# Expert weights loaded by halves over more rounds, and expert rows gathered three ahead, in a sparse-attention and MoE kernel

## The chip, the core and the metric

The kernel runs on one core of one Trainium2 chip. The metric is the device time of one execution in microseconds (us). A profile is one execution; its span begins with the first instruction, and all moments below are us from there. The engines are TensorE (PE, with its weight loads as PEld), VectorE (DVE), ScalarE (ACT), GpSimd (POOL) and SyncE (SP). SP, ACT and POOL issue DMAs, each on queues of its own.

## The reference

Attention over 4 batches of 8 heads, 768 positions of 64. Keys are cut into 24 chunks of 32; each query keeps the 6 chunks with the highest bound, and the result feeds a layer of 8 experts of which each token takes one, at most 80 tokens per expert.

```python
ub = np.sum(np.maximum(q[:, :, :, None, :] * k_min[:, :, None, :, :],
                       q[:, :, :, None, :] * k_max[:, :, None, :, :]), axis=-1)
ub = np.where(causal, ub, -1e9)                       # whole chunks ahead of the query
top_chunks = np.argsort(ub, axis=-1)[..., -6:]
scores = np.where(sel & (pos[:, None] >= pos[None, :]), scale * q @ k.T, -1e9)
x = (softmax(scores) @ v), heads side by side         # 3072 tokens x 512
expert_idx = np.argmax(x @ w_gate, axis=1); gate_w = probs[expert_idx]
for e in range(8):                                    # the 80 tokens with the highest gate
    out[tok_idx] = gate_w[tok_idx, None] * (np.maximum(x[tok_idx] @ w1[e], 0) @ w2[e])
```

Tokens that are dropped have zero rows in `out`.

## The kernel before

**Rounds.** The 32 heads are 8 quads of 4. A quad has 6 rounds, one for each pair of 128-key blocks against a third (256) of the queries, so the attention is 48 rounds, `for rd in range(N + 1)` with `g, r = divmod(rd, 6)`. In a round `score` puts scores into PSUM on PE (L459, and L463 for the chunk penalty), `exps` takes the exponential on ACT (L474), and on diagonal blocks POOL applies the causal mask (L479). On the other rounds (`summed`) POOL adds the two key blocks' exponentials into `both` (`sum_pairs`, L503). `value` multiplies by v (L492), `denom` sums (L517). Both belong to the round before, so PE has the next scores to work on while ACT and POOL are at it. After the last round of a query third `evacuate`, `gate_rows`, `scales` and `rows` divide and compute the gate logits, and `store` writes rows of x to a buffer in DRAM (`x_dram`).

**Bounds.** Each quad prepares the next: keys and queries are transposed on DVE (L264), the chunk minima and maxima taken (L281), keys reordered by POOL (L289), and in round r = 3 (round 4 in the first quad) `bound_all` issues 128 small matmuls (L390) for the bounds, of which `rank_all` makes the penalty. Keys and values of a quad to come are loaded by SP, its queries by ACT.

**Order of work.** The whole loop is under `tc.manual_schedule` for all engines: each engine's instructions run in the order in which the program writes them. In a round POOL has the mask or the pair sum, then what `flush` brings, then the expert weights due in that round, then the preparation steps. ACT issues zero fills of `out` after its exponentials.

**Weights.** Each expert has w1 (512 x 1024) and w2 (1024 x 512) in float32; a POOL DMA casts each to bf16 on the way (1024 KB written to SBUF). Eleven matrices, experts 0 to 4 and w1 of expert 5, go to tiles of their own, in the rounds of `whole_at`, by `load_whole` through `load_parts` (L153). The other five are loaded in rounds 40 to 44 by `late_weights`, in pieces, into tiles that the attention needs no more: `kn`, `qn` (round 40), `kT`, `qT` (41), `qp` (42), `QB`, `KB` (43), `vn` (three pieces, 44). POOL's loads use eight completion counters in turn.

**Zero fills.** `out` is filled with zeros by 12 DMAs of 512 KB (L139) in the rounds of `fills`.

**Experts.** After the selection of each expert's 80 tokens (steps of `freeze` and `weigh`, from round 44 on; the last indices come at L1003 to L1017), the second part of the kernel runs with only PE's order by hand. The lists of POOL, DVE and ACT are left to the scheduler there. POOL gathers the 80 rows of each expert from `x_dram` (L1232, one indirect DMA per expert, all eight first); `turn_rows` transposes them on PE (L1241) and copies them to SBUF on ACT (`XT`, L1244); `hidden` is 32 matmuls (L1255), whose first half goes through the relu on DVE (L1258), the second on ACT (L1261), both into `HT`; `result` is 8 matmuls (L1269), scaled by the gate on DVE (L1272) and scattered to `out` by POOL (L1274). The loop has PE run hidden(e), turn_rows(e+1), result(e-1).

Of the kernel before, what the change touches and what calls it, by code (L numbers as in the profile page):

```python
# [9 lines left out]
BF16 = mybir.dt.bfloat16  # L10
# [3 lines left out]
P = 128  # L14
# [11 lines left out]
NEXP = 8  # L26
DFF = 1024
# [9 lines left out]
def kernel(  # L37
# [11 lines left out]
    nc = tc.nc  # L49
# [93 lines left out]
    weights = {}  # L143
# [9 lines left out]
            nc.gpsimd.dma_start(out=dst, in_=src[:, c0:c0 + n, :])  # L153
            parts += [dst[:, c, :] for c in range(n)]

    def load_whole(e, which):
        w = wpb[which].tile([P, 4 * DFF], BF16, name=("w1", "w2")[which])
        load_parts(e, which, [w[:]])

    NQUAD = NBH // 4  # L160
    THIRD = 2 * P
# [43 lines left out]
    with tc.tile_pool(name="small", bufs=2) as small, \  # L205
# [853 lines left out]
        steps_of = {2: ["K0"], 3: ["K1", "Q0", "Q1"], 6: ["K0", "K1"], 7: ["Q0"], 8: ["Q1"]}  # L1059
        for g in range(2, NQUAD - 1):  # L1060
            steps_of.update({6 * g - 1: ["K0"], 6 * g: ["K1"], 6 * g + 1: ["Q0"], 6 * g + 2: ["Q1"]})
        fills = {11: 1, 17: 1, 23: 1, 29: 1, 45: 2, 46: 3, 47: 3}
        filled = list(range(sum(fills.values())))
        assert len(filled) == NTOK // (2 * P)
        whole_at = (2, 5, 10, 16, 22, 28, 34, 35, 36, 37, 40)
        ends = {}
        fz = freeze()
        frozen = {(N - 4, 2), (N - 4, 1), (N - 3, 1), (N - 2, 0), (N - 2, 1), (N - 1, 0)}
        with tc.manual_schedule(engines=set(mybir.EngineType) - {mybir.EngineType.Unassigned}):
            first, others = slice(0, 2), slice(2, QBLK)  # L1070
            load(0, k4, "kn", first)
            load(0, q4, "qn", first, nc.scalar)
            nc.scalar.activation(out=minus1[:], in_=crow[:], func=mybir.ActivationFunctionType.Exp,
                                 scale=1e-3)
            load(0, k4, "kn", others)
            load(0, q4, "qn", others)
            load_v(0, first)
            nc.sync.dma_start(out=wg_sb[:], in_=moe_w_gate.rearrange("(t r) e -> r t e", r=P))
            load_k(1)
            load_v(0, others)  # L1080
            load_q(1)
            load_v(1)
            idle(24)
            nc.gpsimd.memset(PEN[0][:], 0.0)
            build_indicator(cand[1][:, 0:SEQ])
            u = prep(0)
            units = [u]
            u["turn"]("K", 0)
            u["K"](0)
            build_edge()  # L1090
            u["turn"]("Q", 0)
            u["Q"](0)
            u["bound"](1, 2)
            u["turn"]("K", 1)
            u["K"](1)
            u["rank"](1, 2)
            u["turn"]("Q", 1)
            u["Q"](1)
            u["turn"]("K", 2)
            u["turn"]("Q", 2)  # L1100
            busy(14)
            build = {0: build_constants, 16: build_selection, 22: build_ties}
            for rd in range(N + 1):
                g, r = divmod(rd, 6)
                if r == 1 and 1 <= g < NQUAD - 1:
                    load_v(g + 1)
                if r == (1 if g else 3) and g + 2 < NQUAD:
                    load_k(g + 2)
                if rd - 3 in ends:
                    eg, et = ends[rd - 3]  # L1110
                    scales(eg, et)
                    rows(eg, et)
                    if eg % 2:
                        best(eg // 2, et)
                ps_S = score(rd) if rd < N else None
                if rd - 2 in ends:
                    gate_rows(*ends[rd - 2])
                if rd < N:
                    exps(rd, ps_S)
                    if summed(rd):  # L1120
                        sum_pairs(rd)
                    if rd == 4:
                        flush(bulk)
                if r == (4 if g else 5) and g + 2 < NQUAD:
                    load_q(g + 2, nc.scalar)
                for _ in range(fills.get(rd, 0)):
                    zero_fill(filled.pop(0), nc.scalar)
                flush()
                if rd - 3 in ends and eg == NQUAD - 1:
                    gates(eg // 2, et)  # L1130
                    store(eg // 2, et)
                if rd in build:
                    build[rd]()
                if rd == 0:
                    build_projection()
                if rd in whole_at:
                    load_whole(*divmod(whole_at.index(rd), 2))
                late_weights(rd)
                if rd == 0:
                    units[0]["bound"](2, 4)  # L1140
                    units[0]["rank"](2, 4)
                    units[0]["Q"](2)
                    units[0]["K"](2)
                    busy(5)
                    finish(0)
                    busy(5)
                for kind, f in steps_of.get(rd, []):
                    if (kind, f) == ("K", "0"):
                        units.append(prep(len(units)))
                    units[-1]["step"](kind, int(f))  # L1150
                if rd == 3:
                    flush()
                u = units[min(g + 1, NQUAD - 1)] if len(units) > g + 1 else None
                at = 3 if g else 4
                def sort():
                    for _ in range(pace(rd)):
                        if merges and next(merges[0], merges) is merges:
                            merges.pop(0)

                if r != at:  # L1160
                    sort()
                if (rd, 0) in frozen:
                    next(fz, None)
                if rd == 1:
                    units[0]["bound"](4, 6)
                    units[0]["rank"](4, 6)
                if 1 < rd < N:
                    value(rd - 1)
                    if (rd, 2) in frozen:
                        assert not merges  # L1170
                        next(fz, None)
                    if r == at and g + 1 < NQUAD:
                        u["bound_all"]()
                    if r == 5 and g + 1 < NQUAD:
                        u["unselect"]()
                    finish(rd - 1)
                if r == at and g + 1 < NQUAD:
                    u["rank_all"]()
                if r == at:
                    sort()  # L1180
                if rd != 3:
                    flush(bulk)
                if rd == N - 2:
                    turn_new(0)
                if (rd, 1) in frozen:
                    assert not merges
                    next(fz, None)
                for d in (3, 4):
                    eg, et = ends.get(rd - d, (0, 0))
                    if eg % 2 == 1 and eg < NQUAD - 1 and (et == 0) == (d == 4):  # L1190
                        gates(eg // 2, et)
                        store(eg // 2, et)
                        make = {(3, 0): lanes1, (3, 2): lanes_mid, (5, 1): lanes2,
                                (5, 2): lanes3}.get((eg, et))
                        if make:
                            merges.append(make())
            last = (NQUAD - 1, 2)
            value(N - 1)
            denom(N - 1)
            evacuate(*last)  # L1200
            weigh0()
            turn_new(1, wide("ps_n"))
            gate_rows(*last)
            next(fz, None)
            scales(*last)
            weigh1()
            weigh1_rooms()
            weigh1_own()
            best(NB - 1, 2)
            for run in held_back:  # L1210
                run()
            weigh1_sum()
            gates(NB - 1, 2)
            flush()
            rows(*last)
            store(NB - 1, 2)
            weigh1_late()
            idle(10)
            turn_new(2)
            weigh2()  # L1220

    with tc.tile_pool(name="xp", bufs=8) as xp, \
# [2 lines left out]
         tc.tile_pool(name="psX", bufs=2, space=bass.MemoryType.PSUM) as psX, \  # L1225
         tc.tile_pool(name="psH", bufs=4, space=bass.MemoryType.PSUM) as psH, \
         tc.tile_pool(name="psY", bufs=2, space=bass.MemoryType.PSUM) as psY, \
         tc.manual_schedule(engines={mybir.EngineType.PE}):
        X = []
        for e in range(NEXP):  # L1230
            Xe = xp.tile([CAP, XW], I32, name="X")
            nc.gpsimd.indirect_dma_start(out=Xe[:], out_offset=None, in_=x_dram[:],  # L1232
                                         in_offset=bass.IndirectOffsetOnAxis(ap=gidx[:, e:e + 1], axis=0))
            X.append(Xe)

        XTs = {}

        def turn_rows(e):
# [46 lines left out]
        turn_rows(0)  # L1285
        for e in range(NEXP):
            HT = hidden(e)
            if e + 1 < NEXP:
                turn_rows(e + 1)
            if held is not None:  # L1290
                result(e - 1, held)
            held = HT
# [36 lines left out]
```

## Time and profile before

Three runs: 303.57 us median (302.44 to 303.88). The profiled execution has a span of 301.7 us.

| engine | busy us | share of the span | instructions |
|---|---|---|---|
| PE | 258.9 | 86% | 5149 |
| DVE | 198.2 | 66% | 731 |
| ACT | 153.6 | 51% | 351 |
| POOL | 195.0 | 65% | 394 |

| queue | packets | MB |
|---|---|---|
| q0, issued by POOL | 13536 | 18.67 |
| q1, issued by SP | 37072 | 17.07 |
| q10, issued by ACT | 8576 | 11.27 |

A row of the timeline gives start, busy time, engine, line, operation, output <- inputs with their shapes, the number of instructions, and in brackets the idle time before them with what released them; "issue" there is time in which the engine waited for nothing that the profile shows. A slice line of the page cuts the span into 40 parts of 7.5 us; in PEclk a 9 is full or nearly full clock, a 5 half. MB of q0 are counted as written, after the cast.

Where stages lie in the profile: the bounds of the first quad's successor (round 4) are at 31.8 to 34.2, rounds 40 to 44 at 204 to 228, the last matmuls ahead of the experts' at 256.7 to 259.2, the gathers at 257.7 to 267.2, the expert stage until the end of the span.

### The profile page before, as it was taken

How to read it: one execution, taken by the hardware profiler on the slowest of the kernel's cores; microseconds unless marked ns; L12 is line 12 of the kernel's file. 1: busy time of each engine (PE TensorE's matmuls, PEld its weight loads, DVE VectorE, ACT ScalarE, POOL GpSimd, SP SyncE). 2: the span in 40 equal slices, each digit the busy share in tenths (PEclk: the TensorE clock that was granted, in tenths of full speed). 3: DMA queues.
4: the chain of work that ended last, by engine and by line, in shares of the span. 5: the costliest groups of instructions: out<-in, count | busy, mean ns of one | idle time of the engine just before them, and what ended most of it. 6: DMA issues, size and time to landing. Idle time of an engine off the chain costs nothing. (4 is left out here: it accounts for less than half of the span.)

```text
span 301.7 us, 12390 instructions
## 1 busy us (share of the span) xinstructions
PE 258.9 (86%) x5149; PEld 160.9 (53%) x5149; DVE 198.2 (66%) x731; ACT 153.6 (51%) x351; POOL 195.0 (65%) x394
## 2 busy tenths in 40 slices
PE   8999669979899998989999898969979775629991
PEld 3566335646566565656766555535646442326760
DVE  4769746557748664996988999772888778201431
ACT  1465616836584684658478465804736354012220
POOL 8196707938997993999698389947987201631322
PEclk9999959999999999999999999987999999857998
DMA  6599909939974991998399199997999995110121
GB/s 169 88 211 196 210 11 175 210 76 213 261 162 120 170 216 33 227 220 185 96 203 217 39 193 190 217 198 147 188 210 234 294 296 204 46 44 22 47 64 35
DMA packets 59239, 47.80 MB, mean 158 GB/s; under 512 B 27846, under 2 KB 51526, under 8 KB 59184
## 3 DMA queue, kind: packets, MB, share of 16 engines
q0 software_dynamic: 13536, 18.67, 36.0%
q1 hardware_dynamic: 37072, 17.07, 27.4%
q10 hardware_dynamic: 8576, 11.27, 13.1%
q8 instruction: 40, 0.66, 0.9%
q14 instruction: 15, 0.12, 0.1%
HBM read 53.10 MB, written 10.76 MB: 212 GB/s over the span
## 5 line engine op out<-in xcount | busy, mean ns | idle before, releaser
L474 ACT ACTIVATE E<-ps_S 128x384 f32<-128x384 f32 (+1 forms) x192 | 88.8, 554 | 40.7 <-PE ps_S L463 40.7
L492 PE MATMUL ps_num<-E,vn 128*32 128x256 f32 (+1 forms) x1536 | 86.4, 360 | 3.6 <-POOL E L479 3.4
L503 POOL TENSOR_TENSOR both<-E 128x256 f32<-128x256 f32 x88 | 61.4, 725 | 19.4 <-ACT E L474 19.4
L492 PEld LDWEIGHTS ps_num<-E,vn 128*32 128x32 f32 x1536 | 47.6, 111 | 31.2 <-POOL E L479 5.9
L479 POOL TENSOR_SCALAR_AFFINE_SELECT E<-E 128x256 f32<-128x256 f32 x96 | 42.2, 469 | 29.1 <-ACT E L474 28.9
L459 PE MATMUL ps_S<-QB,KB 32*128 32x256 bf16 (+1 forms) x768 | 35.7, 261 | 3.0 <-issue 3.0
L537 ACT ACTIVATE DSB<-ps_den 128x256 f32<-128x256 f32 x24 | 9.2, 382 | 39.5 <-PE ps_den L533 39.1
L463 PE MATMUL ps_S<-PENT,ind 32*128 32x256 bf16 (+1 forms) x384 | 24.9, 255 | 1.0 <-ACT PENT L419 0.6
L517 PE MATMUL ps_den<-E,ones 128*32 128x256 f32 (+1 forms) x416 | 24.4, 333 | 1.5 <-issue 1.5
L459 PEld LDWEIGHTS <-KB 32*128 32x128 bf16 x768 | 17.2, 93 | 15.6 <-issue 13.5
L289 POOL CAST KB<-kT 128x768 bf16<-128x768 f32 (+1 forms) x20 | 25.3, 1274 | 0.1
L1274 POOL DMA_INDIRECT out_dram<-Y,sidx x8 | 7.4, 922 | 23.1 <-DVE Y L1272 23.1
L517 PE MATMUL ps_den<-both,ones 128*32 128x256 f32 x176 | 16.9, 394 | 5.6 <-issue 5.5
L402 DVE STREAM_TRANSPOSE ub<-ps_u 128x160 f32<-128x160 f32 x28 | 7.3, 318 | 17.9 <-PE ps_u L390 17.9
L547 DVE RECIPROCAL rec<-ps_dT 128x8 f32<-128x8 f32 x24 | 4.8, 202 | 21.6 <-PE ps_dT L545 21.5
L517 PEld LDWEIGHTS ps_den<-E,ones 128*32 128x32 f32 x416 | 13.5, 109 | 8.7 <-issue 3.3
L264 DVE STREAM_TRANSPOSE kT<-kn 128x768 f32<-128x768 f32 (+1 forms) x17 | 15.6, 920 | 3.5 <-DMA kn<-in_k_dram 3.5
L523 ACT ACTIVATE npt<-ps_num 128x512 f32<-128x512 f32 x24 | 14.6, 609 | 6.1 <-PE ps_num L492 6.1
L669 DVE MAX8 cand<-cand 64x8 f32<-64x128 f32 (+3 forms) x40 | 13.7, 343 | 5.2 <-ACT cand L683 4.1
L569 DVE TENSOR_TENSOR x_nat<-ps_xn,rec 128x512 bf16<-128x512 f32 x24 | 16.5, 687 | 0.9 <-PE ps_xn L568 0.8
L298 ACT ACTIVATE qp<-qT 128x640 f32<-128x640 f32 (+2 forms) x20 | 12.4, 641 | 9.2 <-DVE qT L264 9.1
L281 DVE TENSOR_REDUCE KMM<-kT 128x24 f32<-128x768 f32 (+1 forms) x20 | 15.8, 789 | 1.6 <-PE ps_u L355 1.1
(242 smaller groups left out, 463.9 us busy)
## 6 DMA issues: line engine op xcount, KB each, us to landing
w<-in_moe_w_dram POOLq DMA_DIRECT2D x11, 1024.0 KB, 10.3
out_dram<-zero_tile ACTq DMA_DIRECT2D x12, 512.0 KB, 11.2
kn<-in_k_dram SPq DMA_DIRECT2D x28, 192.0 KB, 5.4
vn<-in_v_dram SPq DMA_DIRECT2D x28, 192.0 KB, 7.8
qn<-in_q_dram ACTq DMA_DIRECT2D x24, 192.0 KB, 3.9
x_dram<-x_nat SPq DMA_DIRECT2D x12, 257.0 KB, 6.8
qn<-in_q_dram SPq DMA_DIRECT2D x4, 192.0 KB, 5.3
kn<-in_moe_w_dram POOLq DMA_DIRECT2D x1, 768.0 KB
```

Source lines behind the costliest of these rows:

```text
L264: nc.vector.transpose(out=dst[:, fs, 32 * xs.start:32 * xs.stop].rearrange("p f (x t) -> p x f t", t=CHUNK), in_=src[:].rearrange("p c (i ...
L281: nc.vector.tensor_reduce(out=out_.rearrange("p (c j) -> p c j", j=4), in_=kv, axis=mybir.AxisListType.XY, op=op)
L289: nc.gpsimd.tensor_copy(out=straight(KB[s][:, f, ts]), in_=natural(kT[:, f, ts]))
L459: nc.tensor.matmul(out=ps_S[h][:, m, 0:wid], lhsT=KB[s][rs, w, keys], rhs=QB[s][rs, w, q0:q0 + wid], start=(w == 0), stop=False, skip_grou ...
L463: nc.tensor.matmul(out=ps_S[h][:, m, lo - q0:wid], lhsT=ind[rs, keys], rhs=PENT[s][rs, lo - NFULL:q0 + wid - NFULL], start=False, stop=Tru ...
L474: nc.scalar.activation(out=E[:].rearrange("p m q -> p (m q)")[:, 0:last], in_=ps_S[h][:].rearrange("p m q -> p (m q)")[:, 0:last], func=my ...
L479: nc.gpsimd.affine_select(out=diag, in_=diag, compare_op=ALU.is_ge, fill=0.0, base=0, pattern=[[0, 2], [1, 4], [4, CHUNK]], channel_multip ...
L492: nc.tensor.matmul(out=NUM[q0:q0 + 32, a, c0:THIRD], lhsT=nats[(g, "vn")][:, kb, 2 * a + r, 32 * f:32 * (f + 1)], rhs=Es[rd][2 * a + r][:, ...
L503: nc.gpsimd.tensor_tensor(out=both[:], in0=E[:, 0, :], in1=E[:, 1, :], op=ALU.add)
L517: nc.tensor.matmul(out=dn[32 * h:32 * (h + 1), c0:THIRD], lhsT=ones32[:], rhs=src, start=(i == 0 and m == 0), stop=False, skip_group_check ...
L523: nc.scalar.activation(out=npt[:], in_=NUM[:], func=mybir.ActivationFunctionType.Copy)
L569: nc.vector.tensor_tensor(out=xbuf[(b, t)][:, :, P * gi:P * (gi + 1)].bitcast(BF16).rearrange("p j (k d) -> p j k d", d=HEAD_D), in0=ps_xn ...
```

## The change

Three parts.

1. Weights that go to tiles of their own are loaded in 22 halves of 512 KB instead of 11 wholes of 1024 KB. The rounds are chosen so that none lies in round 2 or in a round with bounds (4, 9, 15, 21, 27, 33, 39). Rounds 34 to 37 had four wholes and have six halves; round 40 had one whole, and rounds 40, 41 and 42 have two halves each. In each round these come ahead of `late_weights`.
2. The zero fills of rounds 11, 17, 23 and 29 move to rounds 12, 18, 24 and 30 (r = 0), and those of rounds 45 to 47 (2, 3, 3) to rounds 44 to 47 (2 each).
3. In the expert stage POOL's order is written by hand too. Three gathers come first; gather e+3 is issued after a one-element copy (`tick`) that reads the first half of HT of expert e, so it cannot start before hidden(e)'s first half has been through DVE.

```diff
-    def load_whole(e, which):
-        w = wpb[which].tile([P, 4 * DFF], BF16, name=("w1", "w2")[which])
-        load_parts(e, which, [w[:]])
+    def load_half(i):
+        which, half = i // 2 % 2, i % 2
+        if half == 0:
+            weights["whole"] = wpb[which].tile([P, 4 * DFF], BF16, name=("w1", "w2")[which])
+        load_parts(i // 4, which, [weights["whole"][:, 2 * DFF * half:2 * DFF * (half + 1)]])
...
-        fills = {11: 1, 17: 1, 23: 1, 29: 1, 45: 2, 46: 3, 47: 3}
+        fills = {12: 1, 18: 1, 24: 1, 30: 1, 44: 2, 45: 2, 46: 2, 47: 2}
...
-        whole_at = (2, 5, 10, 16, 22, 28, 34, 35, 36, 37, 40)
+        half_at = (5, 6, 10, 11, 16, 17, 22, 23, 28, 29, 34, 35, 35, 36, 36, 37, 40, 40, 41, 41, 42, 42)
...
-                if rd in whole_at:
-                    load_whole(*divmod(whole_at.index(rd), 2))
+                for i, at_rd in enumerate(half_at):
+                    if at_rd == rd:
+                        load_half(i)
...
-         tc.manual_schedule(engines={mybir.EngineType.PE}):
+         tc.manual_schedule(engines={mybir.EngineType.PE, mybir.EngineType.Pool}):
         X = []
-        for e in range(NEXP):
+        AHEAD = 3
+        tick = yp.tile([1, 1], BF16, name="tick")
+
+        def fetch(e):
             Xe = xp.tile([CAP, XW], I32, name="X")
...
             X.append(Xe)
 
+        for e in range(AHEAD):
+            fetch(e)
...
             HT = hidden(e)
+            if e + AHEAD < NEXP:
+                nc.gpsimd.tensor_copy(out=tick[:], in_=HT[0:1, 0, 0:1])
+                fetch(e + AHEAD)
             if e + 1 < NEXP:
                 turn_rows(e + 1)
```

## The prediction

> **What bounds the kernel now.** I read the page's slices first, then TensorE's (PE's) timeline wherever its digit falls, then windows, transfers and waits there.
>
> The page's clock slices, four queues and one transfer row:
>
> ```profile
> PEclk9999959999999999999999999987999999857998
> ...
> q0 software_dynamic: 13536, 18.67, 36.0%
> q1 hardware_dynamic: 37072, 17.07, 27.4%
> ...
> q8 instruction: 40, 0.66, 0.9%
> ...
> w<-in_moe_w_dram POOLq DMA_DIRECT2D x11, 1024.0 KB, 10.3
> ```
>
> PE is 86% busy, so time lost on PE is time lost at the end. Its clock falls in three places (slices 6, 27 to 28, 35 to 36). q0 is what GpSimd (POOL) issues, mostly weights, cast on the way; q8 carries instructions: 0.66 MB in 40 packets, 16 KB each. The first fall, on PE's timeline (start, us, instructions, idle before):
>
> ```profile
> 34.13 0.63 PE L517 MATMUL ps_den<-both,ones 128*32 128x256 f32 x6
> 40.22 1.01 PE L517 MATMUL ps_den<-both,ones 128*32 128x256 f32 x2 [5.46 <-issue]
> ```
>
> PE stops between the sixth and eighth matmul of one line, for no operand. In the trace's records it stops where a block of 256 of its instructions ends; the fetch of the next was asked for at 32.14 and began at 37.69, 5.55 us later, where quiet fetches begin after about 1.1. Windows of that stop and after it (columns PE, PEld, DVE, ACT, POOL, PEclk, DMA share, GB/s), then of the second fall:
>
> ```profile
> 34.00:40.20 6.20, 0.77 (x21) 0.15 (x7) 3.66 (x26) 0.79 (x2) 1.49 (x2) 0.74 0.73 135
> 40.20:44.00 3.80, 3.78 (x36) 2.09 (x37) 1.69 (x4) 0.00 (x0) 0.00 (x0) 0.52 0.01 4
> 198.50:201.80 3.30, 0.33 (x8) 0.13 (x10) 3.15 (x26) 0.00 (x0) 1.04 (x5) 0.86 1.21 195
> 201.80:207.70 5.90, 5.90 (x67) 2.99 (x67) 2.64 (x13) 1.92 (x5) 3.52 (x7) 0.50 0.83 149
> ```
>
> While the fetch waits, the DMA engines are busy (0.73; 1.21 at the second); PE then goes on at half clock. The rounds with 128 bound matmuls (L390) use a block up in 2.3 to 3.1 us, so a late fetch shows only there. Rounds 40 to 44, POOL's timeline:
>
> ```profile
> 205.83 0.85 POOL L153 DMA_DIRECT2D w<-in_moe_w_dram  x1
> ...
> 227.05 0.72 POOL L153 DMA_DIRECT2D vn<-in_moe_w_dram  x1 [1.80 <-DMA kT<-in_moe_w_dram]
> 228.29 1.42 POOL L503 TENSOR_TENSOR both<-E 128x256 f32<-128x256 f32 x2 [0.52 <-ACT E L474]
> ```
>
> The last load waits until kT's, eight POOL loads earlier, has landed: 1.80 us, harmless. The third fall, after the selection (timelines of PE, POOL and ACT, lines put together by time):
>
> ```profile
> 261.27 1.45 PE L1255 MATMUL ps_H<-XT,w 128*128 128x80 bf16 x32 [0.57 <-ACT XT L1244]
> 266.29 0.90 POOL L1232 DMA_INDIRECT X<-x_dram,gidx  x1 [0.30 <-issue]
> 269.03 0.44 ACT L1261 ACTIVATE HT<-ps_H 128x320 bf16<-128x320 f32 x1 [7.81 <-remote]
> 269.85 2.29 PE L1255 MATMUL ps_H<-XT,w 128*128 128x80 bf16 x32 [6.85 <-ACT XT L1244]
> ```
>
> hidden(0) ends at 262.7, yet ACT takes its second half at 269.03, "remote". In the records PE's completions come 1.3 and 6.3 us late here and nowhere else in the run; the last comes 0.43 us after the eighth gather has landed (268.58). Eight gathers follow each other every 1.2 us from 257.69.
>
> [...]
>
> **The change part by part.**
>
> Round 2 no longer loads weights. That load was issued at 25.27 and held the DMA engines (by the transfers' records q0's share was 0.99 from 28 to 32) while the k and v loads of the quads to come (q1) got 16 GB/s; q1 then ran until 39.5, over the fetch. Without it q1 ends near 33. The fetch, asked for at 32.14, then takes 1.1 + 1.2 (packet) + 1.3 (until PE runs) = about 3.6 us or somewhat more, ending near 36, not 40.22: gain 4.1 us. [...] 40.2 to 43.8 at half clock did 1.8 us of work at full, gain 1.8. Sum 6, range 3 to 6.5.
>
> Round 28 on: halves lie one to a round instead of a whole in one, and rounds 34 to 37 carry 3 MB, not 4. The stop at 198.51 (3.25 us; fetch asked 195.44, begun 199.52, q0 at 0.91) comes from the round 37 load; with half the bytes in flight it should shrink to 1 to 2 us and save part of the 5.9 us at half clock. I take 2.5 of a possible 5; 0 if a half covers the fetch too.
>
> Issues: 11 more weight issues on POOL. An issue of a whole took 0.85 to 1.03 us, of the smaller loads 0.72 to 0.84, so a half adds about 0.75 net: 8 us of POOL, which is 65% busy. Most lies in rounds where POOL waits for ACT (19.4 us before L503 alone); what waits behind them is the mask (L479) or the pair sum (L503), then PE. I take +1, range 0 to 2. Moving zero fills by a round, I put at nothing: they are on ACT's queue, and before round 40 they replace no wait of PE.
>
> Rounds 40 to 42 get six halves (3 MB) where one whole lay. That matters through POOL's order. In the order of both kernels POOL's loads use eight completion counters in turn, so each waits for the one eight back. Before, the last vn (round 44) waited for kT, the end of the first 3.41 MB. Now it waits for the first half of round 42, the end of the first 5.77 MB. Rate in 207 to 228:
>
> ```profile
> q0 software_dynamic: 2756, 3.94, 111.5%
> ```
>
> 3.94 MB in 21 us: 0.19 MB/us, the queue never empty. So that half lands near 207.3 + 5.77/0.195 + 1.5 = 238.4 (I take 0.195, the steady part), and 240 to 241 with round 44's fills sharing. The loads between wait likewise (the qp loads of round 42 for 2.6 MB, to about 222), so the delay builds up from round 43 on; the last wait sets its end. Behind the last vn on POOL stands the pair sum of round 45, done at 231.1 before; behind that PE's denominator, 232.9 to 233.5. Pair sums (2.8 us) and denominator then end at 242 to 246: the wait of 1.80 becomes about 13, of which some 2.4 were slack. Cost +10.5, range 7 to 12.5, and +1 to 2 for a cold PE after so long a gap (the other two gaps cooled it): +12 together. DVE's sorting, solid from 211.9 to 228.3, hides none of it, as it is done before.
>
> Gathers: three first, each later one after a small POOL copy that reads the HT of expert e. The copy is one element; POOL's small ops near it take 0.2 us. What is queued behind it: gather e+3, then the scatter of expert e-1. Gather e+3 needs to land (2.6 us after issue) before turn_rows(e+3), two expert periods of 3.02 us later: hidden. The scatter is delayed by up to 0.9 us of a gather, in a period of 3.02 that has 2.1 us of POOL idle: hidden. The gain: if PE's completions are held by the train, then with three gathers (landed by about 263.6) hidden(1) starts near 263.9 instead of 269.85: 6 us, plus up to 3 of half clock (2.29 and 3.61 against 1.31 and 1.89), minus new single gathers holding something. I take -6.3, range +2 to -9. The scatters, the same kind of transfer one by one, hold nothing in the trace; that is my reason to expect single gathers harmless.
>
> Sum: -6 - 2.5 + 1 + 12 - 6.3 = about -1.8; with the cold start of the expert stage partly saved as well (-1), -2.8. **300.8 us.**
>
> **The rivals.**
>
> A, the late loads' wait is hidden: if the six halves of rounds 40 to 42 drain faster than 0.195 MB/us or earlier, the wait costs 3, not 12: 303.6 - 2.8 - 9 = 292. For: 291 GB/s flowed in 228 to 253. Against: that includes zero fills without cast; q0 alone did 190 all through.
>
> B, the gathers are not what holds PE, or each single one holds it again: 0 instead of -6.3, so 307, slower. For: nothing in the waits names gathers ("remote" only), and the coincidence with the last landing is one case. Against: 480 other completions are on time.
>
> C, the first stop stays since the k and v loads cover the fetch anyway: -1.5 for -6, so 305.3, slower by 0.6%. For: q1 had 0.72 of the engines in 34 to 40. Against: it was late because of the weights.
>
> **How the numbers follow.** My case 0.47 (301), A 0.17 (292), B 0.25 (307), C 0.11 (305.3). My case has its own spread of some 3 us: 0.36 of it faster than 302.05, 0.10 within 0.5%, 0.01 slower; A is all faster; B 0.02 faster, 0.04 same, 0.19 slower; C 0.01, 0.03 and 0.07. Faster 0.56, same 0.17, slower 0.27. Range 292.5 to 308.5: it leaves out half of A and a little of B.
>
> **What would show it.** Step 1: PE's gap at 34 to 40 under 2 us and slice 6 of the clock at 9. Step 2: the gap near 198 shorter, the clock there above 0.5. Step 3: POOL's last vn waiting about 13 us for a load of w, PE idle before its denominator of round 45. Step 4: ACT's second HT right after hidden(0), no "remote" wait of 7.8 us, gathers between scatters. Wrong if the vn does not wait, if PE stops at block ends in other rounds (halves lie in more rounds), or if hidden(1) still starts only when a gather has landed.

## The result, and the profile after

The changed kernel takes 317.22 us (median of 4 runs, 315.63 to 319.65) against 303.73 us before: ratio 1.0452, 95% interval 1.0371 to 1.0533. It is 13.5 us slower, where 2.8 us faster was predicted. The profiled execution has a span of 315.1 us against 301.7. Some executions of a kernel take over 1.5% longer than its fastest; the ratios leave these out, the medians do not, and the profiles of experiments 5 to 7 and 11 are of such long executions.

The first thing to do with two traces of kernels that do the same work is to cut both at the same events. I cut at ACT's first exponential of rounds 5, 40 and 47 and at the first gather:

| stretch | before, us | after, us | difference | predicted |
|---|---|---|---|---|
| start to round 5 | 44.12 | 38.58 | -5.5 | -6 |
| round 5 to 40 | 159.50 | 162.50 | +3.0 | -1.5 |
| round 40 to 47 | 34.41 | 51.57 | +17.2 | +12, with the next row |
| round 47 to the first gather | 19.66 | 22.58 | +2.9 | |
| first gather to the end | 44.01 | 39.87 | -4.1 | -7.3 |
| sum | 301.7 | 315.1 | +13.4 | -2.8 |

Every stretch but one has the sign that was predicted; the sizes differ. Of the 16 us between the -2.8 predicted and the +13.4 measured, 8.1 lie between round 40 and the first gather, 4.5 in rounds 5 to 40, 3.2 in the last row and 0.5 in the first. In the changed kernel the helper functions stand two lines lower: the pair sum is L505 and the denominator L519.

From the page of the changed kernel, the clock slices, the queue that POOL feeds, the instruction queue and the row of weight loads:

```profile
PEclk9999999999999999999999979599959577977997
...
q0 software_dynamic: 13712, 18.67, 35.4%
...
q8 instruction: 40, 0.66, 0.9%
...
w<-in_moe_w_dram POOLq DMA_DIRECT2D x22, 512.0 KB, 8.2
```

The same bytes flow in both kernels, and instructions still come in 40 packets, 0.66 MB. The early fall of the clock (slice 6 before) is gone; but slices 24 to 34 now have six digits of 5 or 7, where the kernel before had 8 and 7 in slices 27 and 28 and only nines around them.

The first stop, on PE's timeline:

```profile
34.61 0.63 PE L519 MATMUL ps_den<-both,ones 128*32 128x256 f32 x6
36.33 0.59 PE L519 MATMUL ps_den<-both,ones 128*32 128x256 f32 x2 [1.09 <-issue]
```

It lies between the same two matmuls as before and is 1.09 us long instead of 5.46. The prediction's block of 256 shows in the records: the stops of the kernel before with "issue" in rounds 4, 9, 21 and 39 (5.46, 1.51, 1.03 and 2.98 us) lie 1024, 2304 and 3584 recorded PE instructions apart, multiples of 256, and from the packet of q8 in the first stop to that in the last it is 27 packets for 27 x 256 instructions. The next packet of q8 began 5.55 us after PE had started the block ahead of the first stop in the kernel before (37.69 after 32.14), and 1.09 us after it in the changed kernel (33.71 after 32.62), without the load of round 2. In 9 of the 40 blocks of the kernel before and in 11 of the changed kernel's it was 0.93 to 1.25 us, the prediction's 1.1. That PE asks for the next block at that start is my inference: the trace records packets and instructions, no request. Windows of the changed kernel (columns PE, PEld, DVE, ACT, POOL, PEclk, DMA share, GB/s) for this stop, the stop of round 39 with what follows it, and the stretch before and after POOL's long wait:

```profile
34.80:36.40 1.60, 0.51 (x7) 0.07 (x1) 1.53 (x9) 0.47 (x1) 1.19 (x1) 1.00 0.02 6
196.00:199.30 3.30, 0.36 (x8) 0.17 (x10) 3.15 (x26) 0.00 (x0) 1.13 (x5) 0.86 0.87 188
199.30:205.20 5.90, 5.90 (x68) 2.99 (x68) 2.60 (x13) 1.92 (x5) 3.56 (x7) 0.50 0.12 11
236.00:245.00 9.00, 2.57 (x66) 1.53 (x58) 0.81 (x1) 2.05 (x7) 2.23 (x4) 0.88 1.10 271
245.00:255.00 10.00, 9.11 (x72) 4.29 (x76) 3.91 (x19) 2.75 (x6) 5.55 (x17) 0.50 1.18 226
```

The first row keeps its clock (1.00). The second and third are those of 198.5 to 207.7 before: on PE nothing changed, down to the 0.50, though the DMA engines are less busy (0.87 for 1.21, then 0.12 for 0.83). The fourth is new: PE has 2.57 us of work in 9 us while the DMA engines are full; in the fifth PE runs 10 us at half clock. POOL's timeline, and PE's, say why:

```profile
203.28 1.52 POOL L153 DMA_DIRECT2D w<-in_moe_w_dram  x2
...
239.86 0.72 POOL L153 DMA_DIRECT2D vn<-in_moe_w_dram  x1 [5.82 <-DMA qT<-in_moe_w_dram]
243.47 0.72 POOL L153 DMA_DIRECT2D vn<-in_moe_w_dram  x1 [2.89 <-DMA w<-in_moe_w_dram]
244.20 2.77 POOL L505 TENSOR_TENSOR both<-E 128x256 f32<-128x256 f32 x4
...
244.99 2.66 PE L519 MATMUL ps_den<-both,ones 128*32 128x256 f32 x7 [6.43 <-POOL both L505]
...
247.45 0.63 PE L519 MATMUL ps_den<-both,ones 128*32 128x256 f32 x1
```

The same pair sum and denominator in the kernel before:

```profile
228.29 2.79 POOL L503 TENSOR_TENSOR both<-E 128x256 f32<-128x256 f32 x4 [0.52 <-ACT E L474]
...
232.92 0.62 PE L517 MATMUL ps_den<-both,ones 128*32 128x256 f32 x8
```

The last vn does wait for a load of w, as predicted, but is issued at 243.47, 40.2 us after the first load of round 40. Before, the figure was 227.05 - 205.83 = 21.2 us. PE's denominator ends 44.8 us after that first load (248.1 - 203.3), where it was 27.7 (233.5 - 205.8): these 17.1 us are the whole loss of rounds 40 to 47. The transfers from 221 to 244, by queue:

```profile
q0 software_dynamic: 1883, 3.09, 74.0%
q10 hardware_dynamic: 1318, 2.57, 32.3%
```

3.09 MB in 23 us is 0.134 MB/us, not 0.195: q10, the zero fills, took 2.57 MB in the same time. ACT issued three pairs of them 15.0, 24.6 and 33.6 us after the first load, all while POOL waited. The expert stage, timelines of POOL, ACT and PE put together by time:

```profile
277.83 0.91 POOL L1238 DMA_INDIRECT X<-x_dram,gidx  x1 [0.30 <-issue]
280.22 0.44 ACT L1269 ACTIVATE HT<-ps_H 128x320 bf16<-128x320 f32 x1 [1.39 <-PE ps_H L1263]
281.04 2.29 PE L1263 MATMUL ps_H<-XT,w 128*128 128x80 bf16 x32 [0.71 <-ACT XT L1252]
283.40 3.62 PE L1277 MATMUL ps_Y<-w,HT 128*80 128x512 bf16 x8
```

ACT takes the second half of HT right after hidden(0); the "remote" wait of 7.81 us is gone. But hidden(1) and result(0) again last 2.29 and 3.62 us, at half clock (0.50 from 280.3 to 287.1).

### The profile page after: what moved, and what is told of

Read it like the earlier page. It is cut to its first block, busy times and chain, and to the rows that moved or that the text cites. A ratio compares the mean times of both kernels' runs of the same rounds, so it can differ in the third digit from the quotient of the medians.

```text
span 315.1 us, 12411 instructions
## 1 busy us (share of the span) xinstructions
PE 270.7 (86%) x5148; PEld 166.6 (53%) x5149; DVE 200.8 (64%) x731; ACT 153.5 (49%) x351; POOL 202.9 (64%) x410
## 3 DMA queue, kind: packets, MB, share of 16 engines
q10 hardware_dynamic: 8576, 11.27, 12.8%
## 5 line engine op out<-in xcount | busy, mean ns | idle before, releaser
L494 PE MATMUL ps_num<-E,vn 128*32 128x256 f32 (+1 forms) x1536 | 90.6, 372 | 8.1 <-POOL E L481 8.1
L494 PEld LDWEIGHTS ps_num<-E,vn 128*32 128x32 f32 x1536 | 50.5, 114 | 36.0 <-POOL E L481 10.6
L505 POOL TENSOR_TENSOR both<-E 128x256 f32<-128x256 f32 x88 | 61.4, 727 | 12.3 <-ACT E L476 12.2
L519 PE MATMUL ps_den<-E,ones 128*32 128x256 f32 (+1 forms) x416 | 27.1, 353 | 1.0 <-issue 1.0
L519 PE MATMUL ps_den<-both,ones 128*32 128x256 f32 x176 | 19.8, 403 | 8.9 <-POOL both L505 7.5
L461 PEld LDWEIGHTS <-KB 32*128 32x128 bf16 x768 | 17.2, 94 | 15.6 <-issue 13.5
L519 PEld LDWEIGHTS ps_den<-E,ones 128*32 128x32 f32 x416 | 15.1, 117 | 9.1 <-issue 3.9
L153 POOL DMA_DIRECT2D w<-in_moe_w_dram x22 | 17.1, 779 | 0.0
```

The lines of the kernel that those rows point to most:

```text
L461: nc.tensor.matmul(out=ps_S[h][:, m, 0:wid], lhsT=KB[s][rs, w, keys], rhs=QB[s][rs, w, q0:q0 + wid], start=(w == 0), stop=False, skip_grou ...
L494: nc.tensor.matmul(out=NUM[q0:q0 + 32, a, c0:THIRD], lhsT=nats[(g, "vn")][:, kb, 2 * a + r, 32 * f:32 * (f + 1)], rhs=Es[rd][2 * a + r][:, ...
L505: nc.gpsimd.tensor_tensor(out=both[:], in0=E[:, 0, :], in1=E[:, 1, :], op=ALU.add)
L519: nc.tensor.matmul(out=dn[32 * h:32 * (h + 1), c0:THIRD], lhsT=ones32[:], rhs=src, start=(i == 0 and m == 0), stop=False, skip_group_check ...
```

## The experiments

Spans and rows below are those of each run's profiled execution; times are medians against the kernel before on the same chip, whose own median beside them was 302.8 to 303.9 us in all but the last experiment of 7 and 8. The stretches are those of the table above.

**1 to 3: each part alone.** Three kernels, each the kernel before with one part of the diff: the third (`gathers_only`), the first (`weights_only`), the second (`fills_only`).

> The kernel before with the third part alone (POOL's order in the expert stage, three gathers ahead). Theory (the train of eight gathers holds PE's completions): first gather to end of span shrinks from 44.0 us to about 40, as in the changed kernel, hidden(1) starts about 6 us after hidden(0) began to wait before: total about 299.5 us. Rival (the stage only went faster because the late loads had shifted the DMA traffic): no gain, 303.5 us, and the second half of HT is again 6 us late.

298.31 us, ratio 0.9843 (0.9758 to 0.9928). First gather to end: 36.7 us against 44.0, the 7.3 us predicted. Timelines of ACT and PE, put together by time:

```profile
267.38 0.44 ACT L1266 ACTIVATE HT<-ps_H 128x320 bf16<-128x320 f32 x1 [1.40 <-PE ps_H L1260]
268.19 1.31 PE L1260 MATMUL ps_H<-XT,w 128*128 128x80 bf16 x32 [0.71 <-ACT XT L1249]
...
269.48 1.89 PE L1274 MATMUL ps_Y<-w,HT 128*80 128x512 bf16 x8
```

Between hidden(0) and the second half of HT there is no wait for "remote", with the late traffic of the kernel before: the rival falls. In this execution the stretch from round 47 to the first gather was 3.4 us longer than before, with the same instructions in the same order but PE at half clock in part of it (the 32 `value` matmuls from 239.14 on took 2.48 us for 1.51), so its span shows less than the stage gained.

> The kernel before with the first part alone (half loads and their rounds). Theory (the six halves of rounds 40 to 42 delay the loads behind them through the eight counters): all of the loss lies here, rounds 4 to 40 gain 2.5 us, rounds 40 to 47 and the selection lose 17 to 20, expert stage as before: 318 to 321 us. Rival (the zero fills brought forward to round 44 share the DMA engines and make a good part of the delay): 308 to 313 us.

310.40 us, ratio 1.0235 (1.0128 to 1.0341). POOL's timeline:

```profile
236.80 0.72 POOL L153 DMA_DIRECT2D vn<-in_moe_w_dram  x1 [3.58 <-DMA w<-in_moe_w_dram]
```

Rounds 40 to 47 lose 10.6 us, the stretch after it nothing. The last vn is issued 34.8 us after the first load (202.00): for this part alone the prediction's sum, some 35 us and +10.5, was right. Half of the loss that I had put down to this part is elsewhere; the rival's numbers hold.

> The kernel before with the second part alone (zero fills moved). Theory: nothing that can be measured, 303 to 304.5 us, the last vn load of round 44 waits 2 to 4 us instead of 1.8. Rival (fills in round 44 slow the last weight loads so that PE waits): 306 us or more, with a gap on PE before the denominator of round 45.

303.23 us, ratio 1.0011 (0.9981 to 1.0042). POOL's timeline:

```profile
229.72 0.71 POOL L153 DMA_DIRECT2D vn<-in_moe_w_dram  x1 [5.26 <-DMA kT<-in_moe_w_dram]
230.45 2.79 POOL L503 TENSOR_TENSOR both<-E 128x256 f32<-128x256 f32 x4
```

The fills do lengthen the wait, from 1.80 to 5.26 us, more than expected; the slack of some 2.4 us and the small rest hide it. Alone the first, second and third part give +6.6, -0.6 (no difference) and -5.5 us, sum about +0.5. Together they give +13.5. What is missing is an interaction. In the profiles, the changes that the three make alone in rounds 40 to 47 add up to 10.3 us, where the changed kernel lost 17.2.

**4 and 5: the fills beside the late loads.** The changed kernel with the fills of before, and with no late fill ahead of round 46:

```diff
-        fills = {12: 1, 18: 1, 24: 1, 30: 1, 44: 2, 45: 2, 46: 2, 47: 2}
+        fills = {11: 1, 17: 1, 23: 1, 29: 1, 45: 2, 46: 3, 47: 3}   # old_fills
+        fills = {12: 1, 18: 1, 24: 1, 30: 1, 46: 4, 47: 4}          # fills_after_loads
```

> The changed kernel with the zero fills of before (first and third part, not the second). Theory (the fills of round 44 cost only where POOL waits for landings, so the second part is worth nothing alone but 6 to 10 us on top of the first): 303 to 308 us. Rival (first and third part disturb each other): 312 us or more.

308.69 us, ratio 1.0231 (1.0153 to 1.0309): 8.5 us less than the changed kernel (7.6, if each is first taken against the kernel before beside it), just over the expected range. The part that costs nothing alone costs some 8 us on top of the others: the last vn is issued 35.1 us after the first load, and rounds 40 to 47 take 46.5 us instead of 51.6. The first and third part together still give +5.9 where their sum is +1.1; in the profiles 3.3 us of that lie in the expert stage, 40.0 us here and 36.7 in experiment 1, with the clock lower here (0.86 for 0.92).

> The changed kernel with the zero fills of rounds 44 and 45 put to rounds 46 and 47 (four each). Theory (the fills of round 44 halve the rate of the weight queue just while POOL waits for its landings): the queue keeps 0.2 MB/us until the last wait ends, pair sum of round 45 starts near 235 instead of 244.2, and the total falls by 8 to 11 us to 306 to 309 us. Rival (the waits depend on the bytes ahead alone, the fills only fill gaps): under 3 us less, 314 us or more.

307.51 us, ratio 1.0140 (1.0091 to 1.0188), 9.7 us less. The weight queue over 204 to 240:

```profile
q0 software_dynamic: 4460, 6.21, 99.2%
```

POOL's timeline:

```profile
206.59 1.52 POOL L153 DMA_DIRECT2D w<-in_moe_w_dram  x2
...
239.00 0.72 POOL L153 DMA_DIRECT2D vn<-in_moe_w_dram  x1 [1.89 <-DMA w<-in_moe_w_dram]
```

6.21 MB from 206.6 on are 0.19 to 0.2 MB/us, to the end of the window. From first load to last vn it is 32.4 us; the prediction's sum without fills, 1.5 + 5.77/0.195 + 1.5, is 32.6. So the path through the counters and the bytes was sized rightly, and the rate with fills was not. In absolute time the pair sum came at 239.7 rather than near 235, since this execution reached round 40 3.3 us later than the changed kernel's.

**6: what stands behind the waiting loads.** Same loads, bytes and counters, with the vn loads issued two rounds later:

```diff
-            elif rd == 44:
+            elif rd == 46:
                 vspace = bf(nats[(6, "vn")][:])
```

> The changed kernel with the three vn loads of round 44 issued in round 46, behind the pair sum of round 45 and the mask of round 46; same loads, bytes and counters. Theory (the loss is what stands behind the waiting loads on POOL): the waits of 2.2, 5.8 and 2.9 us stay or shrink but hold nothing that PE needs; the PE gap of 6.4 us before the denominator of round 45 goes, rounds 40 to 47 lose 3 to 6 us instead of 17, total 302 to 306 us. Rival (the transfers themselves hold PE, by late fetches or late stores of x): 312 us or more.

304.41 us, ratio 1.0002 (0.9966 to 1.0039): 12.8 us less than the changed kernel, as expected. POOL's timeline:

```profile
236.09 2.78 POOL L505 TENSOR_TENSOR both<-E 128x256 f32<-128x256 f32 x4
...
248.11 0.72 POOL L153 DMA_DIRECT2D vn<-in_moe_w_dram  x1 [2.46 <-DMA w<-in_moe_w_dram]
```

The pair sum of round 45 no longer stands behind the vn loads. Rounds 40 to 47 still lose 6.8 us, a little over the 3 to 6 expected; the loads of rounds 42 and 43 still wait in front of other sums and masks (1.07, 3.86, 1.37 and 3.01 us). With the same bytes under way, most of the loss went with the order on POOL: it is what stands behind the waiting loads that holds PE, not the transfers.

**7 and 8: is it a counter?** Six halves as three wholes, in the same rounds and order; then the same with no late fill ahead of round 46.

```diff
-        load_parts(i // 4, which, [weights["whole"][:, 2 * DFF * half:2 * DFF * (half + 1)]])
+        if i < 16:
+            load_parts(i // 4, which, [weights["whole"][:, 2 * DFF * half:2 * DFF * (half + 1)]])
+        elif half == 0:
+            load_parts(i // 4, which, [weights["whole"][:]])
```

> The changed kernel with the six halves of rounds 40 to 42 as three wholes in the same rounds: same bytes in the same order, three POOL loads fewer. Theory (each load waits for the one eight back, through the counters): the last vn then waits for qT, the end of the first 5.24 MB, not 5.77, the waits in rounds 42 and 43 vanish (the loads eight back are the small or earlier ones), and the pair sum of round 45 starts 3 to 6 us earlier than at 244.2: 311 to 314 us. Rival (the waits are for bytes in the queue, whatever the number of loads): no earlier, 316 us or more.

314.86 us, ratio 1.0313 (1.0215 to 1.0411). POOL's timeline:

```profile
241.31 0.72 POOL L153 DMA_DIRECT2D vn<-in_moe_w_dram  x1 [5.80 <-DMA kT<-in_moe_w_dram]
247.21 0.72 POOL L153 DMA_DIRECT2D vn<-in_moe_w_dram  x1 [5.18 <-DMA qT<-in_moe_w_dram]
```

The loads named are those eight back, as expected, and the qp loads no longer wait. But the last vn comes 39.7 us after the first load (207.55), against 40.2: the expected 3 to 6 us did not come. As POOL waits less in rounds 42 and 43, the rounds that follow, and their fills, come earlier: ACT's timeline has three pairs of fills within 26 us of the first load here, while the changed kernel issues its third pair after 33.6 us. Hence the second kernel:

> The changed kernel with both edits: three wholes in rounds 40 to 42 instead of six halves, and no zero fills before round 46. Theory (each load waits for the one eight back; the wholes alone gained nothing only because their earlier rounds brought the fills forward): the last vn waits for qT, the end of 5.24 MB at 0.2 MB/us, and is issued 29 to 30 us after the first load of round 40, where halves with late fills took 32.4 us; total 1 to 4 us under the 307.5 us of that kernel. Rival (the number of loads does not matter): 32 us or more from the first load, total as there.

The last vn is issued 30.2 us after the first load (231.93 - 201.69), against 32.4 us with halves. That is 2.2 us for three loads fewer at the same bytes, nearly as expected, and against the rival. The total can't be laid beside the 307.5 us: this chip ran the kernel before in 297.75 us. The ratio is 1.0192 (1.0040 to 1.0345) against 1.0140, which shows no gain.

**9: the late halves moved earlier.** In the changed kernel:

```diff
-        half_at = (5, 6, 10, 11, 16, 17, 22, 23, 28, 29, 34, 35, 35, 36, 36, 37, 40, 40, 41, 41, 42, 42)
+        half_at = (5, 6, 10, 11, 12, 16, 17, 18, 22, 23, 24, 28, 29, 30, 34, 34, 35, 35, 36, 36, 37, 40)
```

> The changed kernel with five of the six halves of rounds 40 to 42 moved earlier: rounds 12, 18, 24, 30 take one each and round 34 one more, round 40 keeps one. Theory (the wait of POOL's last loads for the bytes ahead of them): PE's gap of 6.4 us before the denominator of round 45 is gone, rounds 40 to 47 take as long as before, about 298 us (295 to 301). Rival (half loads in more rounds hold up instruction fetches or POOL, wherever they lie): stays above 304 us, with new gaps on PE in rounds 10 to 35.

307.78 us, ratio 1.0150 (1.0014 to 1.0285). Rounds 40 to 47 take 33.1 us, less than before: that half of the theory holds. But rounds 5 to 40 lose 12.2 us, as the rival said. The two longest of its stops, on PE's timeline in rounds with bounds, make 5.1 of it:

```profile
116.53 0.75 PE L392 MATMUL ps_u<-qp,KMM 32*32 32x160 f32 x8 [2.88 <-issue]
173.88 0.65 PE L392 MATMUL ps_u<-qp,KMM 32*32 32x160 f32 x31 [2.23 <-issue]
```

**10 and 11: keeping what gains.** The kernel before with the third part, and of the first part one move only; then a second move.

```diff
-        whole_at = (2, 5, 10, 16, 22, 28, 34, 35, 36, 37, 40)
+        whole_at = (5, 6, 10, 16, 22, 28, 34, 35, 36, 37, 40)   # round2_moved
+        whole_at = (5, 6, 10, 16, 22, 28, 29, 34, 35, 36, 40)   # round37_moved
```

> The kernel before with the third part, and of the first part only this: the whole load of round 2 goes to round 6 (rounds 5, 6, 10, 16, 22, 28, 34 to 37, 40), zero fills as before. Theory (the early gain of 6 us and the gain of the gathers add up where nothing is moved to rounds 40 to 42): 292 to 294 us, PE gap at 34 us down to 1.5 us. Rival (the load in round 6 makes a stop elsewhere): 296 us or more, with a stop of PE near rounds 7 to 9.

294.82 us, just over the expected 292 to 294, ratio 0.9706 (0.9558 to 0.9853): faster than both kernels. PE's timeline:

```profile
35.97 0.59 PE L517 MATMUL ps_den<-both,ones 128*32 128x256 f32 x2 [2.04 <-issue]
60.76 0.41 PE L517 MATMUL ps_den<-E,ones 128*32 128x128 f32 x4 [2.81 <-issue]
```

The first stop shrinks to 2.04 us and the load in round 6 costs 2.81 us in round 9 (1.51 before): the rival's stop exists, but is small. Rounds 40 to 47 take 33.9 us, half a us less than before, since nothing was moved there.

> The kernel with the load of round 2 in round 6 and three gathers ahead (294.8 us), with the whole load of round 37 moved to round 29 as well. Theory (the stop of 3.2 us in round 39 comes from the weight queue's backlog, still at 0.91 of the engines when the fetch is asked for): the stop shrinks to 1.5 us or less and half clock after it is avoided, 291 to 293 us. Rival (the fetch there is late whatever lies in the queue, or the load in round 29 stops PE in round 33): 294.5 us or more.

299.60 us, ratio 0.9820 (0.9729 to 0.9911): no better, though the intervals overlap. The stop of round 39, on PE's timeline:

```profile
201.42 0.28 PE L459 MATMUL ps_S<-QB,KB 32*128 32x256 bf16 x2 [2.98 <-issue]
```

It is as long as ever (2.98 us in the kernel before too), although in the 3.8 us up to the start of that fetch, 195.1 to 198.9, the weight queue had 0.61 of the engines (0.92 before, 195.4 to 199.5), with 0.55 (0.24) for q1, loads of SP and stores of x. After it the clock stayed full this time (1.00 from 201.4 to 207.3; the 32 `value` matmuls took 1.91 us, in the kernel before 3.64). The theory for this stop falls: thinning the weights alone does not clear the way.

**12: the length of the train of gathers.**

```diff
-        AHEAD = 3
+        AHEAD = 5
```

> The kernel before with the third part, but five gathers in the first train instead of three. Theory (PE's completions are held while a train of more than three gathers is in flight): the second half of HT of expert 0 is late until about 0.4 us after the fifth gather has landed, 2.5 to 3 us less late than with eight, and the total is 300 to 302 us, between three and eight. Rival (only the POOL order matters, not the length of the train): as with three, about 298 us.

302.45 us, a little over the expected 300 to 302, ratio 0.9977 (0.9941 to 1.0013): no difference in the total. First gather to end: 41.7 us, between 36.7 (three) and 44.0 (eight). ACT's timeline:

```profile
266.68 0.44 ACT L1266 ACTIVATE HT<-ps_H 128x320 bf16<-128x320 f32 x1 [5.06 <-remote]
```

The wait is back, 5.06 us after 7.81 with eight and none with three. PE's completion of that half is late by 0, 3.7 and 6.3 us with three, five and eight gathers.

## Why the prediction was wrong

**The step that failed is the rate** in "lands near 207.3 + 5.77/0.195 + 1.5 = 238.4 (I take 0.195, the steady part), and 240 to 241 with round 44's fills sharing". I took the rate from a stretch of the kernel before in which no fills ran, and allowed the fills about 2 us. They took a third of the queue's rate (0.134 MB/us) from 221 on, for as long as POOL waited. First load to last vn came to 40.2 us in place of some 35, and the pair sum of round 45 ended 43.7 us after the first load instead of 25.3: 18.4, less 2.4 of slack, is 16 us where I had 10.5. Experiments 4 and 5 show this as the term: with the fills later, first load to last vn is 35.1 and 32.4 us, and the total drops by 8.5 and 9.7 us. It is the largest single miss, not the only one: in these two kernels, where the fills no longer come early, 300.8 us would still have been 7 to 8 us too low.

**"Moving zero fills by a round, I put at nothing"** was right for the change alone (experiment 3) and wrong beside the late loads. I costed each edit against the kernel before, not against the other edits. That is a fault of the prediction's design, not of a number: the second part met a wait that the first part created.

**The cold clock after that wait** I took at 1 to 2 us. PE did run at half clock after it (0.50 in the window 245 to 255), but in rounds 40 to 47 that cost about 1 us: 16 us of the 17.2 are the late pair sum, and the denominator behind it ends 17.1 us late. The stretch up to the first gather lost another 2.9 us, part of it to this cold start (its first matmuls, `value` of round 46, take 2.79 us for 1.51). That the long wait is the cause is not shown: the kernels of experiments 1 and 9 lost 3.4 us in the same stretch, in experiment 1 also with half clock in it (2.48 us for 1.51), and their rounds 40 to 47 took 34.0 and 33.1 us, with no long wait at all.

**The mechanism was right**: which load waits for which (POOL's timelines above, experiments 7 and 8; in the records of the kernel before POOL's 22 weight loads use semaphores 111 to 118 in turn, and each from the ninth on waits for the one that the load eight back had), and that what stands behind it on POOL is what costs (experiment 6).

**Step 1, the early stop**, was right: -5.5 for -6, slice 6 of the clock at 9. That a shorter stop would keep the clock was an estimate of mine. It held for this one of 1.09 us (1.00 from 34.8 to 40), while in round 36 of the same execution the clock fell to 0.50 after a wait of 1.74 us.

**Step 2, the stop of round 39**, failed: 2.5 expected, nothing gained. "With half the bytes in flight it should shrink" supposed that the weight queue is what keeps the engines full. Experiment 11 has it at 0.61 and the stop unchanged. What the fetch waits for there is not settled. Full engines from several queues together fit, but no run cleared them all, and against it stands the first stop of the changed kernel, where q1 alone had 0.92 of the engines (32.62 to 33.71) and the fetch began after 1.09 us. Nor does the trace show what made the fetch of the first stop 4.4 us late (5.55 for 1.1): from 30 to 37.7 in the kernel before one packet took 0.17 us on q0 and 0.05 us on q1 in the mean. That busy engines delay a fetch was my estimate from the two stops.

**The issues**, +1, came to about +2. POOL's and PE's timelines of the changed kernel in round 12:

```profile
69.95 0.82 POOL L153 DMA_DIRECT2D w<-in_moe_w_dram  x1
...
72.47 1.69 POOL L481 TENSOR_SCALAR_AFFINE_SELECT E<-E 128x256 f32<-128x256 f32 x4
...
72.97 1.25 PE L494 MATMUL ps_num<-E,vn 128*32 128x256 f32 x18 [1.75 <-POOL E L481]
```

A half load stands ahead of the mask, and PE waits 1.75 us where it waited 0.92; so too in round 24 (2.09 for 1.23) and round 36 (1.74 for 1.25). These three waits, the only ones of PE on POOL over 0.5 us in rounds 10 to 38, add up to 5.6 us, 3.4 before. PE also ran at half clock (0.50) from 181.3 to 184.7, after the third of them, where the kernel before kept full clock; with 3.4 us of work in it, that is 1.7 us at most. What is left of the +3.0 can't be told from the spread: over rounds 5 to 40, the changed kernel and those of experiments 2, 4 and 8, with the same loads in the first 39 rounds, came out 1.8 to 3.0 us above the kernel before, and three kernels with the loads of before 0.1 below to 1.9 above it.

**The gathers** were right: -7.3 with the cold start, and experiment 1 has -7.3. In the changed kernel 4.1 is left, as hidden(1) and result(0) ran at half clock: 2.29 and 3.62 us against 1.31 and 1.89 in experiment 1, 2.7 us. Both executions have a stretch at half clock, from 261.6 to 265.1 in experiment 1, ahead of hidden(0), and from 280.3 to 287.1 in the changed kernel, over hidden(1) and result(0). Why it lies there in one and not in the other is open. "Hidden" was not quite right of the scatters: the timeline of experiment 1 has completions of PE up to 2.6 us late where a scatter and a gather follow within 3 us, and a PE gap of 1.48 us.

**The rivals**: none came. A needed a faster queue, B is refuted by experiments 1 and 12, C by the first stop. All three left out that the fills slow the late loads.

## What to carry to other kernels

Before moving loads into a busy stretch, list what stands behind each on its issuing engine, and size the wait with the rate that the queue will have there, with what the other queues of the new kernel move at the same time (here 2.57 MB of fills on q10, with the weight queue at 0.134 MB/us for 0.195). Cost edits in pairs where one makes a wait and the other adds traffic to it: parts worth +6.6, nothing and -5.5 us gave +13.5 together. When a change mixes gains and losses, take it apart: the two edits that gain, alone, gave 0.9706.

## What the runs showed of the hardware that was not expected

- A train of gathers holds back PE's completions, and the more of them the longer: 0, 3.7 and 6.3 us for three, five and eight. Nothing in the waits names them. What in the chip does it was not tried.
- Zero fills from another engine's queue cut the casting weight queue from 0.19 MB/us (207 to 228 in the kernel before, 190 GB/s in all) to 0.134 MB/us (221 to 244 in the changed kernel), while the engines' total rose to 259 GB/s.
- The stop of round 39 was 2.98 us of idle time in the kernel before and in experiment 11, and 2.94 us in the changed kernel, with different weight loads ahead of it (q0 at 0.92 of the engines in the kernel before, 0.61 in experiment 11).
- The length of a stop of PE did not settle what the clock did. It stayed full after 1.09, 1.75 and 2.09 us in rounds 4, 12 and 24 of the changed kernel, after 2.81 us in round 9 of experiment 10 (the next 8 score matmuls took 0.40 us, 0.61 at half clock in the kernel before) and after 2.98 us in round 39 of experiment 11; it fell to half after 1.74 us in round 36 of the changed kernel (0.50 from 181.3 to 184.7). At the stop of round 39 it went to half for 6.8 us in the kernel before (200.9 to 207.7) and in the changed kernel (198.4 to 205.2).
